# One expert's early block widened from 128 to 160 rows, and the next expert's weight loads and splits issued at other places

## The chip, the cores and the metric

The kernel runs on one core of a Trainium2 chip. The metric is device time in microseconds (us). A core has five engines with a queue each: TensorE (PE in the profile, its weight loads PEld), VectorE (DVE), ScalarE (ACT), GpSimd (POOL) and SyncE (SP), which issues most of the DMA transfers here. Times below are counted from the start of the profiled span.

## The reference

Attention with a local window and a few global keys (2 x 8 heads, 768 positions, head size 64) feeds a dense block, `g = h * tanh(softplus(h))` between a 512 x 2048 and a 2048 x 512 matrix, and that feeds a mixture of eight experts, which is the part that the change touches:

```python
logits = x @ w_gate                          # 1536 tokens, 8 experts
expert_idx = np.argmax(logits, axis=1)
for e in range(E):
    mask = expert_idx == e
    xe = x[mask]
    h = np.maximum(xe @ w1[e], 0.0)          # 512 -> 1024
    ye = h @ w2[e]                           # 1024 -> 512
    out[mask] = gate_w[mask, None] * ye
```

## The kernel before

The tokens stand in six blocks of 256. While the dense block works on its last pass, each finished block is routed: a small product with `w_gate`, a rank within the expert, and two indirect DMAs (scatters, L578) that write the block's rows into the table `xg` in DRAM, sorted by expert. Then the experts run one after another, the fullest first. Each has a fixed capacity, `CAPS = [336, 288, 256, 224, 208, 200, 184, 176]` rows.

The work on experts is a list of stages, `STG`: (expert by rank, first row, rows). The first expert has two stages, an early one of the first `EARLY = 128` rows and one of the other 208; each further expert has one. The fullest expert is fixed after the fifth block, so the early stage starts before the sixth and last block is routed: its rows of the table are there already. The second stage needs rows of the last block, so its loads (`b_xload(1)`) wait for the last scatters.

A stage has eight steps m. `b_L1(g, m)` multiplies the rows by a 128-wide slice of the expert's first matrix and takes the relu; `b_L2(g, m - 2)` multiplies the result by the slice of the second matrix, two steps later (`LAG = 2`). `b_xload` loads the stage's rows (tile `xr`), and `b_xprep` transposes them on TensorE (`btp`) and copies them to `xc`. Stage 0 multiplies in plain float32 with unsplit weights (tile `w0f`), and its relu result is `hf`. All later stages use weights and rows split into a high and a low part: a load (`b_raw`, tile `bst`, eight chunks of 512 KB for an expert), then `b_conv`, which for each of a chunk's two halves casts the high part on ScalarE (L154) and subtracts on VectorE (L155). In a stage of fewer than 256 rows a product is a pair of matmuls: the high weights times high and low rows side by side (L710, 2 x rows columns), and the low weights times the high rows (L711). Then the relu piece takes four instructions: ScalarE copy `t`, VectorE add `t`, ScalarE relu `hc`, VectorE subtract `hc`. `b_yevac` and `b_yout` take the sums out of PSUM, transpose them back (`ytp`) and scatter them to `out`.

A scheduler turns this program order into one queue per engine: an instruction that is ready sooner by its estimate may be put ahead of an earlier one. `tc.issue_after(ins)` puts what its block contains behind `ins`; it acts on the instructions of the engine that `ins` is on, and on no other. Tiles called `xr`, `x` (the routed rows of a block) and `z` share three buffers.

Of the kernel before, what the change touches and what calls it, by code (L numbers as in the profile page):

```python
# [1 line left out]

# [6 lines left out]
F32 = mybir.dt.float32  # L9
# [22 lines left out]
CAPS = [336, 288, 256, 224, 208, 200, 184, 176]  # L32
CAPMAX = max(CAPS)
NWARM = 12
EARLY = 128
ROW = DM + 2
NOID = 65536.0
ERS = NT + 128
# [3 lines left out]
def moe_kernel(ctx, tc, q, k, v, n_global, n_local, w_in, w_out, w_gate, w1, w2, out, dbg=None):  # L42
# [544 lines left out]
    def route_step(blk):  # L587
        if blk not in rsteps:
            rsteps[blk] = route_steps([xes.pop(2 * blk), xes.pop(2 * blk + 1)], ps,
                                      [wk.tile([128, 4, 128], F32, tag="cv", name="xt") for _ in range(2)])  # L590
        sc = next(rsteps[blk], None)
        if sc and blk >= NBLK - 2:
            tc.declare_no_dep(sc[1].ins, sc[0].ins, reason="disjoint rows")
            xdep[:] = [x.ins for x in sc]
# [47 lines left out]
    def b_reg(r):  # L642
        src = permt[0][0:1, r:r + 1] if r else perm0
        ereg[r] = nc.sync.value_load(src, min_val=0, max_val=NE - 1)
# [16 lines left out]
    def b_conv(r, i):  # L661
        which, f, kk = CH[i]
        if kk == 0:
            pool, tag = (wp, "w") if nsw[0] % 6 != 3 else (wlate[0], "w2")
            nsw[0] += 1
            sw[r, which, f] = [pool.tile([128, 4, 512], F32R, tag=tag, name="bw") for _ in range(2)]
        hi, lo = sw[r, which, f]
        st = braw.pop((r, i))
        for k2 in range(2):
            kx = 2 * kk + k2  # L670
            split(st[:, k2, :], hi[:, kx, :], lo[:, kx, :])

    def b_xload(g):
        r, o, cap = STG[g]
        nt = (cap + 127) // 128
        rows = []
        for i in range(nt):
            n = min(128, cap - i * 128)
            xr = xe.tile([128, ROW], F32, tag="x2", name="xr")
            ld = nc.sync.dma_start(xr[0:n], xg[bass.ds(ereg[r] * ERS + o + i * 128, n), :])  # L680
            if g < 2:
                for d in xdep:
                    tc.add_manual_dep(ld.ins, d.name, mybir.DependencyInfo(
                        mybir.DependencyClass.Sync, mybir.DependencyReason.DATA), reason="rows of the scatter")
            rows.append((xr, n))
        bx[g] = rows
# [28 lines left out]
            nc.tensor.matmul(o[:, 0:cap], lhsT=wl, rhs=xh, start=False, stop=last)  # L715

    hcs = {}
    bacc = {}

    def b_L1(g, m):  # L720
        r, _, cap = STG[g]
        cat = cap < 256
        xc = bx[g][2]
        hp = ps.tile([128, 512], F32, tag="b", name="bhp")
        if g == 0:
            hf = wk.tile([128, cap], F32, tag="gh", name="hf", bufs=3)
            for kk in range(4):
                nc.tensor.matmul(hp[:, 0:cap], lhsT=w0f[1, m // 4][:, kk, (m % 4) * 128:(m % 4) * 128 + 128],
                                 rhs=xc[:, kk, :], start=(kk == 0), stop=(kk == 3))
            nc.scalar.activation(out=hf, in_=hp[:, 0:cap], func=AF.Relu)  # L730
            hcs[g, m] = hf
            return
        wh, wl = sw[r, 1, m // 4]
        cs = slice((m % 4) * 128, (m % 4) * 128 + 128)
        for kk in range(4):
            mm3(hp, cap, cat, wh[:, kk, cs], wl[:, kk, cs], xc[:, kk, 0, :], xc[:, kk, 1, :],
                xc[:, kk].rearrange("p a c -> p (a c)"), kk == 0, kk == 3)
        if cat:
            hc = wk.tile([128, 2, cap], F32R, tag="gh", name="hc", bufs=3)
            hh, hl = hc[:, 0], hc[:, 1]  # L740
            hc = hc.rearrange("p a c -> p (a c)")
            t1 = wk.tile([128, cap], F32, tag="e", name="t1")
            nc.scalar.copy(t1, hp[:, cap:2 * cap])
            nc.vector.tensor_add(t1, t1, hp[:, 0:cap])
            src = t1
        else:
            hc = None
            hh = wk.tile([128, cap], F32R, tag="gh", name="hh", bufs=3)
            hl = wk.tile([128, cap], F32R, tag="gl", name="hl", bufs=3)
            src = hp[:, 0:cap]  # L750
        nc.scalar.activation(out=hh, in_=src, func=AF.Relu)
        nc.vector.scalar_tensor_tensor(out=hl, in0=src, scalar=0.0, in1=hh.bitcast(F32),  # L752
                                       op0=ALU.max, op1=ALU.subtract)
        hcs[g, m] = (hh, hl, hc)

    def b_L2(g, m):
        r, _, cap = STG[g]
        cat = cap < 256
        if m == 0:
            bacc[g] = [ps.tile([128, 512], F32, tag="b", name="bacc") for _ in range(4)]  # L760
        if g == 0:
            hf = hcs.pop((g, m))
            for d in range(4):
                nc.tensor.matmul(bacc[g][d][:, 0:cap], lhsT=w0f[2, m // 4][:, m % 4, d * 128:(d + 1) * 128],
                                 rhs=hf, start=(m == 0), stop=(m == 7))
            return
        hh, hl, hc = hcs.pop((g, m))
        wh, wl = sw[r, 2, m // 4]
        for d in range(4):
            mm3(bacc[g][d], cap, cat, wh[:, m % 4, d * 128:(d + 1) * 128],  # L770
                wl[:, m % 4, d * 128:(d + 1) * 128], hh, hl, hc, m == 0, m == 7)
# [347 lines left out]
    NM = 8 * len(STG)  # L1119
    LAG = 2  # L1120
    YLAG = LAG + 1
    for i in range(NM + YLAG + 1):
        g, m = divmod(i, 8)
        if i < NM:
            r = STG[g][0]
            b_L1(g, m)
            if m == 0 and g + 1 < len(STG) and STG[g + 1][0] != r:
                b_reg(r + 1)
            if m == (0 if g else 3) and g + 1 < len(STG):
                b_xload(g + 1)  # L1130
            if m == 5 and g + 1 < len(STG):
                b_xprep(g + 1)
            if g > 0 and r + 1 < NE:
                if m == 1:
                    b_raw(r + 1, 0)
                    b_raw(r + 1, 1)
                    b_raw(r + 1, 2)
                if m >= 2 and m + 1 < 8:
                    b_raw(r + 1, m + 1)
        if i >= LAG and i - LAG < NM:  # L1140
            g2, m2 = divmod(i - LAG, 8)
            b_L2(g2, m2)
            if m2 == 7:
                b_yevac(g2)
        if i == 0:
            with tc.high_priority():
                route_step(LAST)
                route_step(LAST)
                final_rank()
            routed = dsi_ins[0].ins  # L1150
        if i < 8:
            with tc.issue_after(routed):
                b_conv(0, i)
        if i < NM and g > 0 and r + 1 < NE and m >= 2:
            b_conv(r + 1, m - 2)
        if i < NM and g > 1 and m in (0, 1):
            b_conv(r, m + 6)
        if i >= YLAG and (i - YLAG) % 8 == 7:
            b_yout((i - YLAG) // 8)
# [217 lines left out]
```

## Time and profile before

| | us |
|---|---|
| median of 3 runs (lowest, highest) | 628.48 (628.40, 630.04) |
| the profiled execution, its own time | 628.33 |
| its span | 626.5 |
| TensorE busy in the span | 590.0 (94%) |
| VectorE, ScalarE, GpSimd busy | 485.2, 394.6, 90.1 |

The busy shares are means over stages with different limits. The stage to look at here lies between 400 and 455 us, where the last block is routed and the first expert's two stages run; after it TensorE is busy without a break to the last expert. The granted clock is given as a share of TensorE's full speed: 1.00 is 2.4 GHz, 0.50 is 1.2 GHz.

### The profile page before, as it was taken

What the parts mean: (1) busy time and instruction counts of PE and PEld (TensorE: products, weight loads), DVE (VectorE), ACT (ScalarE), POOL (GpSimd) and SP (SyncE); (2) the same over time, 40 slices, a digit from 0 to 9 for tenths busy, and PEclk for the clock granted to TensorE, in tenths of its full rate; (3) what the DMA queues carried; (4) which work ended last, traced back from release to release, by engine and by line L of the source; (5) the groups of instructions that cost most, each with busy time, mean ns of one, the idle gap of its engine ahead of it and who ended that gap; (6) DMA issues with size and microseconds to landing.
All of it is one profiled execution on the core that took longest, in us unless ns stands there. A gap on an engine that the chain in (4) does not pass through costs nothing.

```text
span 626.5 us, 11976 instructions
## 1 busy us (share of the span) xinstructions
PE 590.0 (94%) x4214; PEld 511.3 (82%) x4214; DVE 485.2 (77%) x1250; ACT 394.6 (63%) x965; POOL 90.1 (14%) x152
## 2 busy tenths in 40 slices
PE   5988999999999999999999999877999999999991
PEld 4555676766799999998989898677999999998991
DVE  5798998999799999867767777565875677987741
ACT  2689998989867665555565546363754566776530
POOL 2201000100000101000211201142211122221111
PEclk7599999999999999999999999996999999999996
DMA  7686655647999764431421210546667376568000
GB/s 217 204 268 190 210 175 196 208 152 259 244 308 380 230 202 149 165 101 35 132 88 52 102 35 35 176 169 219 242 236 250 103 278 218 184 240 298 30 17 20
DMA packets 54872, 109.93 MB, mean 175 GB/s; under 512 B 5674, under 2 KB 12842, under 8 KB 54802
## 3 DMA queue, kind: packets, MB, share of 16 engines
q1 hardware_dynamic: 49122, 90.18, 44.1%
q0 software_dynamic: 5680, 18.89, 9.1%
q8 instruction: 35, 0.57, 0.4%
q14 instruction: 35, 0.29, 0.1%
HBM read 84.64 MB, written 25.10 MB: 175 GB/s over the span
## 4 chain that ended last, share of the span: by engine, by line
PE 84%; DMA 5%; DVE 3%; ACT 3%; issue 2%; POOL 1%; SPq 0%; DVEq 0%; POOLq 0%; ACTq 0%
PE hp L427 23%; PE acc L446 20%; PE bacc L710 6%; PE bhp L710 6%; PE av L379 4%; PE sp L288 4%; PE bhp L711 3%; PE bacc L711 3%; PE pt L348 2%; PE pt L350 2%; DMA xg<-x,dsi 1%; PE ytp L797 1%; DMA xr<-xg 1%; PE bacc L713 1%; PE bhp L713 1%
## 5 line engine op out<-in xcount | busy, mean ns | idle before, releaser
L427 PE MATMUL hp<-xh,wpair 128*128 128x256 f32 x768 | 154.4, 288 | 1.0 <-ACT xh L391 1.0
L427 PEld LDWEIGHTS hp<-xh,wpair 128*128 128x128 f32 x768 | 122.5, 189 | 8.4 <-issue 3.6
L446 PE MATMUL acc<-wpair,gh 128*128 128x512 f32 x384 | 124.8, 401 | 1.4 <-ACT gh L483 1.4
L427 PE MATMUL hp<-xl,wpair 128*128 128x256 f32 x384 | 110.4, 288 | 0.3 <-DVE xl L396 0.3
L155 DVE TENSOR_TENSOR bw<-bst,bw 128x512 fp32r<-128x512 f32 x112 | 73.0, 685 | 11.6 <-ACT bw L154 10.6
L446 PEld LDWEIGHTS acc<-wpair,gh 128*128 128x128 f32 x384 | 68.2, 188 | 16.3 <-issue 3.5
L446 PE MATMUL acc<-wpair,gl 128*128 128x512 f32 x192 | 77.2, 403 | 0.0
L154 ACT CAST bw<-bst 128x512 fp32r<-128x512 f32 x112 | 64.6, 620 | 19.1 <-PE bhp L714 7.9
L427 PEld LDWEIGHTS hp<-xl,wpair 128*128 128x128 f32 x384 | 72.3, 188 | 5.0 <-issue 3.2
L454 ACT ACTIVATE e<-hp 128x512 f32<-128x512 f32 x48 | 28.8, 601 | 69.6 <-PE hp L427 69.6
L710 PE MATMUL bacc<-hc,bw 128*128 128x416 f32 (+4 forms) x192 | 60.1, 366 | 0.4 <-DVE hc L752 0.4
L710 PE MATMUL bhp<-xc,bw 128*128 128x416 f32 (+4 forms) x192 | 60.4, 367 | 0.0
L320 ACT ACTIVATE P<-P,mx 128x232 f32<-128x232 f32 (+1 forms) x96 | 44.8, 470 | 11.1 <-DVE mx L302 10.9
L711 PE MATMUL bhp<-xc,bw 128*128 128x208 f32 (+4 forms) x192 | 48.9, 255 | 0.0
L711 PE MATMUL bacc<-hc,bw 128*128 128x208 f32 (+4 forms) x192 | 48.8, 254 | 0.0
L464 DVE SCALAR_TENSOR_TENSOR n<-n,r 128x512 f32<-128x512 f32 x48 | 33.0, 688 | 18.7 <-ACT r L462 18.5
L302 DVE CUSTOM_DVE_ANT_0 P<-sp,ndist 128x232 f32<-128x232 f32 (+1 forms) x96 | 35.7, 374 | 10.3 <-PE sp L288 9.4
L446 PEld LDWEIGHTS acc<-wpair,gl 128*128 128x128 f32 x192 | 36.1, 188 | 9.3 <-issue 2.7
L486 DVE SCALAR_TENSOR_TENSOR gl<-n,gh 128x512 fp32r<-128x512 f32 x48 | 33.1, 689 | 11.5 <-ACT gh L483 10.6
L288 PE MATMUL sp<-kT,qT 64*128 64x232 f32 (+1 forms) x192 | 35.6, 428 | 3.1 <-DVE qT L263 3.1
L379 PE MATMUL av<-PT,vv 128*64 128x128 f32 (+2 forms) x384 | 36.0, 303 | 2.0 <-ACT PT L357 2.0
L710 PEld LDWEIGHTS bacc<-hc,bw 128*128 128x128 f32 x192 | 36.1, 188 | 1.3 <-DVE hc L752 0.6
(188 smaller groups left out, 1294.6 us busy)
## 6 DMA issues: line engine op xcount, KB each, us to landing
bst<-in_moe_w_dram SPq DMA_DIRECT2D x56, 512.0 KB
wst<-in_moe_w_in_dram SPq DMA_DIRECT2D x16, 512.0 KB
wst<-in_moe_w_out_dram SPq DMA_DIRECT2D x16, 512.0 KB
xl<-xs POOLq DMA_DIRECT2D x12, 512.0 KB, 4.1
xh<-xs POOLq DMA_DIRECT2D x12, 512.0 KB, 4.8
xpl<-xps SPq DMA_DIRECT2D x24, 256.0 KB
xg<-z SPq DMA_DIRECT2D x24, 224.9 KB
w0f<-in_moe_w_dram SPq DMA_DIRECT2D x8, 512.0 KB
```

The lines of the kernel that those rows point to most:

```text
L154: nc.scalar.copy(hi, src)
L155: nc.vector.tensor_sub(lo, src, hi.bitcast(F32))
L288: nc.tensor.matmul(sp[:, 0:w], lhsT=qT[r, p_, :], rhs=kT[r, p_, k0:k0 + w], start=True, stop=True)
L302: nc.vector.tensor_tensor_reduce(out=P[:, j, 0:w], in0=sp[j][:, 0:w], in1=ndist[:, d0:d0 + w], scale=-(2.0 ** -(h + 1)), scalar=3.0e38, op ...
L320: nc.scalar.activation(out=P[:, j, 0:w], in_=P[:, j, 0:w], func=AF.Exp, bias=mx[:, j:j + 1], scale=-1.0, accum_out=su[:, j:j + 1])
L379: nc.tensor.matmul(av[64 * j:64 * j + 64, p_, :], lhsT=lh, rhs=rh, start=(c == 0), stop=(c == 1))
L427: yield lambda f=f, kk=kk, wi=wi, xx=xx, cs=cs: nc.tensor.matmul(hp[:, f, :], lhsT=w[:, wi, kk, cs], rhs=xx[:, kk, :], start=(kk == 0 and ...
L446: yield lambda f=f, o=o, cs=cs, gi=gi, wi=wi, first=first, last=last: nc.tensor.matmul(accs[b][o], lhsT=gi[:, cs], rhs=w[:, wi, f, :], sta ...
L464: nc.vector.scalar_tensor_tensor(out=n, in0=n, scalar=0.25, in1=r, op0=ALU.add, op1=ALU.mult)
L486: nc.vector.scalar_tensor_tensor(out=gl, in0=n, scalar=-(2.0 ** -80), in1=gh.bitcast(F32), op0=ALU.mult, op1=ALU.subtract)
L710: nc.tensor.matmul(o[:, 0:2 * cap], lhsT=wh, rhs=xc, start=first, stop=False)
L711: nc.tensor.matmul(o[:, 0:cap], lhsT=wl, rhs=xh, start=False, stop=last)
```

## The change

`EARLY` is 160, so that the stages of the first expert have 160 and 176 rows in place of 128 and 208. Stage 0 is written out as a block of its own. In it the second stage's transposes (`b_xprep(1)`) stand behind all eight `b_L1` and six `b_L2`, and six of the second expert's eight weight loads are issued there; before they stood in stage 1. The splits of the second expert's weights stand in stage 1 as before, now each within `issue_after(hlast[m - 2])`, where `hlast[m]` is the VectorE instruction that ends stage 1's relu piece m.

```diff
-EARLY = 128
+EARLY = 160
...
-        nc.vector.scalar_tensor_tensor(out=hl, in0=src, scalar=0.0, in1=hh.bitcast(F32),
-                                       op0=ALU.max, op1=ALU.subtract)
+        ins = nc.vector.scalar_tensor_tensor(out=hl, in0=src, scalar=0.0, in1=hh.bitcast(F32),
+                                             op0=ALU.max, op1=ALU.subtract)
+        if g == 1:
+            hlast[m] = ins.ins
...
-    for i in range(NM + YLAG + 1):
+    def early_block():
+        for m in range(8):
+            b_L1(0, m)
+            if m == 3:
+                b_xload(1)
+            if m >= LAG:
+                b_L2(0, m - LAG)
+            if m == 0:
+                with tc.high_priority():
+                    route_step(LAST)
+                    route_step(LAST)
+                    final_rank()
+            with tc.issue_after(dsi_ins[0].ins):
+                b_conv(0, m)
+        b_xprep(1)
+        b_reg(1)
+        for i in range(6):
+            b_raw(1, i)
+        for m in range(8 - LAG, 8):
+            b_L2(0, m)
+        b_yevac(0)
+
+    early_block()
+    for i in range(8, NM + YLAG + 1):
...
-            if m == (0 if g else 3) and g + 1 < len(STG):
+            if m == 0 and g + 1 < len(STG):
                 b_xload(g + 1)
...
+                if m in (3, 4) and g == 1:
+                    b_raw(r + 1, m + 3)
...
-        if i < NM and g > 0 and r + 1 < NE and m >= 2:
-            b_conv(r + 1, m - 2)
+        if i < NM and r + 1 < NE and m >= 2:
+            with tc.issue_after(hlast[m - 2]) if g == 1 else nullcontext():
+                b_conv(r + 1, m - 2)
```

TensorE's queue at the second stage's transposes, before. `L728` is a product of stage 0's first matrix, `L764` of its second, `L697` a transpose of the second stage's rows, `L710` and `L711` that stage's first pair.

```order
L764 MATMUL bacc<-hf,w0f 128x128 x4
L697 MATMUL btp<-ident,xr 128x128 x4
L764 MATMUL bacc<-hf,w0f 128x128 x2
L697 MATMUL btp<-ident,xr 128x80 x4
L728 MATMUL bhp<-xc,w0f 128x128 x4
L764 MATMUL bacc<-hf,w0f 128x128 x2
L728 MATMUL bhp<-xc,w0f 128x128 x4
L764 MATMUL bacc<-hf,w0f 128x128 x4
L710 MATMUL bhp<-xc,bw 128x416
```

The same place in TensorE's queue now; the two kinds of product of stage 0 are `L729` and `L767` here.

```order
L729 MATMUL bhp<-xc,w0f 128x160 x4
L767 MATMUL bacc<-hf,w0f 128x160 x4
L697 MATMUL btp<-ident,xr 128x128 x4
L697 MATMUL btp<-ident,xr 128x48 x4
L767 MATMUL bacc<-hf,w0f 128x160 x8
L710 MATMUL bhp<-xc,bw 128x352
```

Of stage 0's 64 products 40 stood ahead of the transposes and 56 do now; 8 are left behind them, the last two steps of the second matrix.

ScalarE's queue at the end of stage 0, before. `L730` is the relu of stage 0, `L702` the copy of the second stage's transposed rows, `L154` a cast, of the first expert's weights where it reads `w0f` and of the second expert's where it reads `bst`.

```order
L154 CAST bw<-w0f 128x512 x2
L702 CAST xc<-btp 128x4x128
L154 CAST bw<-w0f 128x512
L702 CAST xc<-btp 128x4x80
L154 CAST bw<-w0f 128x512
L730 ACTIVATE hf<-bhp 128x128 x2
L154 CAST bw<-bst 128x512 x2
L743 COPY t_5385<-bhp 128x208
```

The same place in ScalarE's queue now (`L731` is the relu of stage 0, `L788` the copy of its sums, `L744` the first copy of stage 1's relu piece).

```order
L731 ACTIVATE hf<-bhp 128x160
L154 CAST bw<-w0f 128x512
L154 CAST bw<-bst 128x512 x2
L731 ACTIVATE hf<-bhp 128x160
L154 CAST bw<-bst 128x512 x2
L731 ACTIVATE hf<-bhp 128x160
L702 CAST xc<-btp 128x4x128
L702 CAST xc<-btp 128x4x48
L788 COPY ys<-bacc 128x160 x2
L744 COPY t_5432<-bhp 128x176
```

Four casts of the second expert's weights moved from behind the last two relus of stage 0 and the copies to `xc` to ahead of them.

SyncE's queue from the second stage's row loads, now; the second expert's loads stood behind three more `xr` loads before.

```order
L680 DMA xr<-xg 48x514
L644 TENSOR_LOAD perm
L644 ISA x2
L656 ISA
L656 DMA bst<-in_moe_w_dram 128x2x512
L656 ISA
L656 DMA bst<-in_moe_w_dram 128x2x512
L658 ISA
L658 DMA bst<-in_moe_w_dram 128x2x512
```

The weight loads now follow the second stage's own rows, and the three row loads of the second expert follow the weights.

## Rows read from the trace of the kernel before

**Rows 1.** Chain that ended last, routing of the last block (start us, us, what)

```profile
418.19 5.97 DMA xg<-x,dsi
...
424.42 2.88 DMA xr<-xg
```

**Rows 2.** TensorE's timeline (start us, us, engine, line, op, tiles, count, [idle before, releaser])

```profile
406.02 0.63 PE L697 MATMUL btp<-ident,xr 128*128 128x128 f32 x4 [1.02 <-DMA xr<-xg]
...
408.91 0.39 PE L728 MATMUL bhp<-xc,w0f 128*128 128x128 f32 x2
...
416.90 1.06 PE L764 MATMUL bacc<-hf,w0f 128*128 128x128 f32 x8
...
418.69 1.06 PE L764 MATMUL bacc<-hf,w0f 128*128 128x128 f32 x8
427.34 1.11 PE L697 MATMUL btp<-ident,xr 128*128 128x128 f32 x4 [7.60 <-DMA xr<-xg]
...
434.04 0.44 PE L710 MATMUL bhp<-xc,bw 128*128 128x416 f32 x1
...
454.64 0.31 PE L713 MATMUL bhp<-xc,bw 128*128 128x288 f32 x1
```

**Rows 3.** Stretches (us, busy of each engine, granted clock, DMA share, GB/s)

```profile
422.00:422.50 0.50, 0.00 (x0) 0.00 (x0) 0.00 (x0) 0.00 (x0) 0.05 (x1) 0.65 0.00 0
...
427.34:432.30 4.96, 4.96 (x25) 4.96 (x26) 3.19 (x6) 2.32 (x5) 1.91 (x8) 0.50 0.55 147
...
434.04:454.64 20.60, 20.60 (x147) 20.28 (x146) 16.74 (x37) 14.92 (x37) 3.63 (x5) 1.00 0.76 267
```

**Rows 4.** TensorE's waits from 434 to 615 us (us in total, times, longest)

```profile
PE bacc L710 <- DVE hc L752: 0.4, 1, 0.4
```

**Rows 5.** TensorE's timeline, pairs at 208 and 176 rows, and transposes

```profile
437.32 0.26 PE L711 MATMUL bhp<-xc,bw 128*128 128x208 f32 x1
...
441.35 0.26 PE L711 MATMUL bhp<-xc,bw 128*128 128x208 f32 x1
...
443.16 0.26 PE L711 MATMUL bacc<-hc,bw 128*128 128x208 f32 x1
...
447.18 1.40 PE L697 MATMUL btp<-ident,xr 128*128 128x128 f32 x12
...
600.08 0.24 PE L711 MATMUL bacc<-hc,bw 128*128 128x176 f32 x1
...
601.17 0.24 PE L711 MATMUL bhp<-xc,bw 128*128 128x176 f32 x1
```

**Rows 6.** SyncE's timeline, issues of row and weight loads

```profile
425.03 0.34 SPq L680 DMA_DIRECT2D xr<-xg  x1
...
430.51 0.38 SPq L656 DMA_DIRECT2D bst<-in_moe_w_dram  x1
...
431.10 0.38 SPq L656 DMA_DIRECT2D bst<-in_moe_w_dram  x1
...
431.68 0.99 SPq L658 DMA_DIRECT2D bst<-in_moe_w_dram  x2
```

**Rows 7.** SyncE's register load by its line (ns min/median/max, first to last start)

```profile
L644 SPq TENSOR_LOAD <-perm x1: 273/273/273, 425.4 to 425.4; - x1
```

**Rows 8.** ScalarE's timeline, casts of the second expert's weights

```profile
434.33 1.14 ACT L154 CAST bw<-bst 128x512 fp32r<-128x512 f32 x2 [0.57 <-DMA bst<-in_moe_w_dram]
...
435.74 0.62 ACT L154 CAST bw<-bst 128x512 fp32r<-128x512 f32 x1
...
438.05 1.14 ACT L154 CAST bw<-bst 128x512 fp32r<-128x512 f32 x2 [0.88 <-DMA bst<-in_moe_w_dram]
439.10 0.33 ACT L743 COPY t<-bhp 128x208 f32<-128x208 f32 x1
```

**Rows 9.** ScalarE's and VectorE's timelines, rows of stage 1

```profile
428.50 0.58 ACT L702 CAST xc<-btp 128x512 fp32r<-128x512 f32 x1 [8.23 <-PE btp L697]
...
429.11 0.69 DVE L703 TENSOR_TENSOR xc<-btp,xc 128x512 fp32r<-128x512 f32 x1 [7.93 <-ACT xc L702]
```

More of the change, by code (lines that the diff above doesn't have):

```diff
@@ L1 @@
-from contextlib import ExitStack
+from contextlib import ExitStack, nullcontext
 import concourse.bass as bass
@@ L717, in moe_kernel @@
     hcs = {}
+    hlast = {}
     bacc = {}
@@ L1126, in moe_kernel @@
             b_L1(g, m)
-            if m == 0 and g + 1 < len(STG) and STG[g + 1][0] != r:
+            if m == 0 and g > 1 and g + 1 < len(STG):
                 b_reg(r + 1)
-            if m == (0 if g else 3) and g + 1 < len(STG):
+            if m == 0 and g + 1 < len(STG):
                 b_xload(g + 1)
@@ L1132, in moe_kernel @@
                 b_xprep(g + 1)
-            if g > 0 and r + 1 < NE:
-                if m == 1:
+            if r + 1 < NE:
+                if m == 1 and g > 1:
                     b_raw(r + 1, 0)
@@ L1137, in moe_kernel @@
                     b_raw(r + 1, 2)
-                if m >= 2 and m + 1 < 8:
+                if m >= 2 and m + 1 < 8 and g > 1:
                     b_raw(r + 1, m + 1)
-        if i >= LAG and i - LAG < NM:
+                if m in (3, 4) and g == 1:
+                    b_raw(r + 1, m + 3)
+        if i - LAG >= 8 and i - LAG < NM:
             g2, m2 = divmod(i - LAG, 8)
@@ L1144, in moe_kernel @@
                 b_yevac(g2)
[L1145 to L1153, printed above, removed]
-        if i < NM and g > 0 and r + 1 < NE and m >= 2:
-            b_conv(r + 1, m - 2)
+        if i < NM and r + 1 < NE and m >= 2:
+            with tc.issue_after(hlast[m - 2]) if g == 1 else nullcontext():
+                b_conv(r + 1, m - 2)
         if i < NM and g > 1 and m in (0, 1):
```

## The prediction

> **What bounds the kernel now.** I read the page's busy shares first, then TensorE's timeline around the first expert, the chain of waits there, and the stretches with the granted clock. TensorE works nearly all the time, so what counts is where it waits. The largest wait behind the attention is one place: its timeline stops when the product that starts at 418.69 is through, at about 419.6, and goes on at 427.34, after 7.60 us idle, with the transposes of stage 1's rows [rows 2]. The chain says what it waits for: the second scatter of the last block (418.19, 5.97 us) and then the load of the rows that it wrote (424.42, 2.88 us) [rows 1]. The stretches show a second price: the granted clock falls in the half microsecond from 422.0, and all work from 427.34 to 432.30, 5.0 us of it, runs at 0.50, which is 1.2 GHz; from 434.04 it is 1.00 again [rows 3]. From there to the end TensorE has no break to speak of: in stage 1 it is busy for all of the 20.60 us from 434.04 to 454.64, and one wait of 0.4 us for a relu piece stands later [rows 3, 4]. Hence what is gained or lost up to stage 2's first matmul, at 454.64 before, should reach the end nearly whole.
>
> **Wider early block.** The starts at 416.90 and 418.69 lie 16 records of stage 0's products apart: 0.112 us a record, two records a product, 0.224 us for 128 columns [rows 2]. No row shows 160 columns of this kind. Bounds: nothing more, if the pace is set by something that each record costs whatever its width (transposes of 128 and 32 rows come at 1.40 / 12 = 0.117 us each alike [rows 5]), or in proportion, 0.280 us. I take the proportion, because the pairs of the later stages get shorter with fewer columns. The Trainium skill (FP8 and Floating Point Precision, TensorE Precision Notes) says that true float32 takes four passes through the array; by it 32 more columns would add an estimated 0.053 us a product, close to the upper bound; no run here shows the width yet.
>
> TensorE now runs 56 products ahead of the transposes in place of 40. Before, 40 products (8.96 us) and the router's small products filled 408.91 to 419.6, so the router's share is 1.7 us. Now: 56 x 0.280 = 15.7, plus 1.7, from about 409.3: done at 426.7 (423.5 by the lower bound). That is before the rows can be there, so the width costs nothing on the path: the wait for the rows hides it, and only the last 8 products (2.2 us) are left behind it.
>
> **The early rows come in two tiles.** Four more transposes (0.12 us each [rows 5]) stand before the dense block's last matmuls, and with these the last block's routing, its scatters and the rows of stage 1 move by the same 0.4 us. The second tile's load may cost up to 0.6 more, the spacing of two such issues (424.42 to 425.03 [rows 1, 6]); its 32 rows follow 128 that TensorE already waited 1.02 us for [rows 2]. I take 0.4: rows there at 427.7, transposes of 128 and 48 rows (8 x 0.117) done at 428.7. The wait ahead of them is 1.0 us, in place of 7.6.
>
> **What is late next.** The second expert's first loads leave SyncE behind the second row load. That was issued at 425.03 and a register load followed at 425.4, 0.27 us long [rows 6, 7]; with the 0.4 of above it ends at 426.1, and an issue takes another 0.4 (0.38 [rows 6]): first chunk issued at about 426.5, the second 0.6 later (430.51 to 431.10). Before, the first took from 430.51 to the cast at 434.33, 3.8 us, and the second at most 4.6 us (431.10 to 435.74) [rows 6, 8]. So they land at about 430.3 and by 431.7.
>
> These landings did not matter before. Now ScalarE's queue has their four casts ahead of the last two relus of stage 0 and of the copies to `xc`; the hold acts on VectorE's half of the split alone. That ScalarE does not look past a waiting cast is seen before: the casts at 438.05 waited 0.88 us for their chunk, and the copy behind them started at 439.10, as the casts ended, though the matmuls that it copies were through at 437.6 [rows 5, 8]. The Trainium skill (TensorE: Matmul & The Clock Gate, Architectural detail) calls the queues of ScalarE and VectorE strict FIFO, which speaks against this change; by a queue that is not, the time would be that of the third rival below, and the trace agrees with the page.
>
> Step by step, a pair of casts being 1.14 us, a relu some 0.2 (a copy of more columns 0.33 [rows 8]), and the copy and subtraction of the rows 0.6 and 0.7 [rows 9]: casts of the first chunk 430.3 to 431.4, relu 6 at 431.6; casts of the second 431.7 to 432.8, relu 7 at 433.0; copies to `xc` until 433.8 and VectorE behind them: stage 1 can start at 434.4. TensorE idles from 428.7 to 431.6, then has two times 1.1 us of stage 0 to do.
>
> **Shorter stage 1.** Pairs start 1.81 / 6 = 0.302 us apart at 208 rows and 1.09 / 4 = 0.273 at 176 [rows 5]. Of 64 pairs 56 lie ahead of stage 2's first matmul: 15.3 us, with 12 transposes of the next rows (1.4) and eight of the way back (0.6): 17.3 us from stage 1's start. Before, the 20.60 us held these and the last 8 products of stage 0. The last 8 pairs save 0.2 more. VectorE was busy 16.74 of the 20.60 us [rows 3], gets 0.7 us of extra output scaling and loses about 0.6 in narrower pieces, so it has 16.8 to do in 17.3 us and what it may finish later; I cost it at nothing, and up to 1 us if that cover is too thin.
>
> **Sum at full clock.** Stage 2 starts at 434.4 + 17.3 = 451.7, against 454.64: 2.9, and 0.2: 3.1 us less, 625.2 us from the profiled execution's 628.33.
>
> **The clock.** Before, it fell some 2.5 us into the idle time and came back 5.0 us after work resumed [rows 2, 3]. Now two idle times of 1.0 and 2.9 us have 1.0 us of transposes between them. If it falls in the second, TensorE does the two steps at half speed, 431.6 to 436.0, and has full speed from 436.6: as if stage 1 had started at 436.3. That leaves 1.2 us of gain: 627.1. If it does not fall, 625.2 stands. The idle time is about as long as the one that was enough before, so I take the middle, 626.1; by the median, 0.15 above the profiled execution, 626.2.
>
> **Rivals.**
> - Weights land sooner. The row load, of half the bytes, took 2.88 us [rows 1]. If the chunks do too, relu 6 comes at 430.7, the idle time is 2.1 us, shorter than the time after which the clock fell, and stage 1 starts at 433.3: 4.2 us less, 624.1. For it speaks that fewer row loads run beside them, against it that a chunk has twice the bytes of the row tile.
> - Weights land late: slower than before. With six chunks in the air the third one took 6.4 us before (431.68 to 438.05 [rows 6, 8]). If the first now takes that, it lands at 432.9, relu 6 comes at 434.2 and, at half clock, stage 1 starts as if at 438.9: stage 2 at 456.2, less 0.2, is 1.4 us later, 629.7. It decides from a first landing some 5.0 us after issue. Against it: the first chunk has no other chunk ahead of it.
> - The hold keeps the casts back on ScalarE as well, or it looks past them. Then relus 6 and 7 are done early, TensorE goes on from the transposes at 428.7 to the last 8 products and starts stage 1 at 430.9 at full clock: stage 2 at 448.2, 6.6 us less, 621.7. The queue's order speaks against it.
>
> **How the numbers follow.** The held casts, 625.2 to 627.1, have 0.62, early weights 0.18, late weights 0.16, casts out of the way 0.04. A change of 0.3%, 1.9 us, is about what a measurement of this kernel can tell from none. Faster by more: 0.58 of the first case, all of the second and fourth: 0.58. Slower by more needs over 630.4, beyond the third case's 629.7: 0.05. Within: 0.37. The range leaves out the fourth case, a little of the second and most of the third: 623.4 to 628.8. The likeliest case's own range is 625.0 to 627.3.
>
> **What would show it.** In the changed profile the 7.60 us wait for `xr` should be about 1 us, with 56 products ahead of it, at 0.28 us each. A new wait of about 3 us should stand between the transposes and the next product, released by the relu `hf`, and ScalarE should show a wait for `bst` with the relu and the copies right behind the casts. Stage 1's first pair should start between 434 and 436.5, its pairs 0.27 us apart, and stage 2 between 451.5 and 453.6. The clock should be 0.50 for less time than the 10 us of before. It is wrong if TensorE goes on from the transposes without a wait for `hf`, if stage 1 loses time to VectorE, or if the rows of the last block come over 1 us later.

## The result, and the profile after

The changed kernel takes 623.47 us (median of 20 runs; 628.36 before, of 20). The ratio of the two is 0.9912, with a 95% interval of 0.9884 to 0.9939: by the ratio 5.5 us less, between 3.8 and 7.3. The forecast was 626.2, 2.2 us less. Medians here are of all runs; the ratios leave the slow ones out.

Executions of both kernels spread over several microseconds: their profiles have spells of different length in which the granted clock stands at 1.2 GHz, in the first 80 us, in attention work that the change doesn't touch. The profiled execution of the changed kernel, 627.95 us long, has one from 36.5 to 49 us that the profile of before lacks. So this document compares one stretch that lies behind these spells: from the last block's first transposes (`tp`, L533) to stage 2's first matmul. TensorE's timeline of the kernel before, and then of the changed one, has it so:

```profile
407.72 1.35 PE L533 MATMUL tp<-ident,x 128*128 128x128 f32 x8
```

```profile
413.56 0.60 PE L533 MATMUL tp<-ident,x 128*128 128x128 f32 x4
...
429.84 1.25 PE L729 MATMUL bhp<-xc,w0f 128*128 128x160 f32 x8
430.93 1.25 PE L767 MATMUL bacc<-hf,w0f 128*128 128x160 f32 x8
432.02 0.97 PE L697 MATMUL btp<-ident,xr 128*128 128x128 f32 x8
433.59 2.64 PE L767 MATMUL bacc<-hf,w0f 128*128 128x160 f32 x16 [0.60 <-ACT hf L731]
436.35 0.43 PE L710 MATMUL bhp<-xc,bw 128*128 128x352 f32 x1
...
450.30 0.43 PE L710 MATMUL bhp<-xc,bw 128*128 128x352 f32 x1 [0.53 <-DVE bw L155]
```

Stage 2 starts at 454.64 before [rows 2] and at 454.72 now, so the stretch is 46.92 us before and 41.16 now: 5.76 less, as much as the runs measured. The wait of 7.60 us for `xr` [rows 2] is gone altogether: the transposes follow the products without a gap. A wait of 0.60 us for `hf` is new, and one of 0.53 in stage 1 for VectorE's subtraction of weights.

The clock does not fall. The stretches of the changed kernel (TensorE, its weight loads, VectorE, ScalarE, GpSimd busy; granted clock; DMA) show 1.00 where it was 0.50 for five microseconds before [rows 3], and 0.50 only in the spell near the start:

```profile
36.50:49.00 12.50, 12.35 (x52) 8.78 (x51) 8.33 (x36) 5.38 (x18) 1.23 (x2) 0.50 0.56 182
...
426.00:433.59 7.59, 6.99 (x54) 6.70 (x52) 4.89 (x10) 3.23 (x9) 2.10 (x4) 1.00 0.74 228
436.35:454.72 18.37, 17.84 (x132) 17.34 (x133) 15.37 (x35) 11.30 (x30) 4.18 (x12) 1.00 0.72 236
```

The chain that ended last answers to [rows 1]: the second scatter's piece is 4.70 us long in place of 5.97, and behind it stands the weight load for `bst` in place of the rows' load. The rows' load now ends while TensorE still has products:

```profile
419.98 1.18 POOL xg L578
421.16 0.30 issue
421.46 4.70 DMA xg<-x,dsi
...
428.22 3.90 DMA bst<-in_moe_w_dram
```

Why the rows are sooner stands in GpSimd's timeline, which the prediction did not read. Before, the two scatter instructions of the last block are these:

```profile
414.32 3.56 POOL L578 DMA_INDIRECT xg<-x,dsi  x1 [7.95 <-issue]
418.19 3.86 POOL L578 DMA_INDIRECT xg<-x,dsi  x1 [0.30 <-issue]
```

In the changed kernel:

```profile
419.98 1.18 POOL L578 DMA_INDIRECT xg<-x,dsi  x1 [7.41 <-DVE dsi L577]
421.46 2.52 POOL L578 DMA_INDIRECT xg<-x,dsi  x1 [0.30 <-issue]
```

7.42 us have become 3.70, and the edit does not name these instructions. The experiments ask why.

ScalarE's queue behaves as forecast: the casts wait for their chunk, and relu and copies stand behind them.

```profile
432.20 1.14 ACT L154 CAST bw<-bst 128x512 fp32r<-128x512 f32 x2 [4.36 <-DMA bst<-in_moe_w_dram]
433.25 0.29 ACT L731 ACTIVATE hf<-bhp 128x160 f32<-128x160 f32 x1
433.49 1.14 ACT L154 CAST bw<-bst 128x512 fp32r<-128x512 f32 x2
434.53 0.30 ACT L731 ACTIVATE hf<-bhp 128x160 f32<-128x160 f32 x1
434.73 0.80 ACT L702 CAST xc<-btp 128x512 fp32r<-128x512 f32 x2
```

### The profile page after: what moved, and what is told of

Same layout as the page of the kernel before. It is cut to its first block, busy times and chain, and to the rows that moved or that the text cites. A ratio compares the mean times of both kernels' runs of the same rounds, so it can differ in the third digit from the quotient of the medians.

```text
span 625.7 us, 12000 instructions
## 1 busy us (share of the span) xinstructions
PE 596.0 (95%) x4222; PEld 514.8 (82%) x4222; DVE 484.8 (77%) x1251; ACT 394.9 (63%) x966; POOL 82.7 (13%) x155
## 4 chain that ended last, share of the span: by engine, by line
PE 78%; DVE 7%; DMA 6%; ACT 4%; issue 3%; POOL 1%; SPq 0%; DVEq 0%; POOLq 0%; ACTq 0%
PE hp L427 23%; PE acc L446 20%; PE av L379 4%; PE sp L288 4%; PE bhp L710 4%; PE bacc L710 4%; DMA bst<-in_moe_w_dram 3%; DVE bw L155 2%; PE pt L348 2%; PE bhp L711 2%; PE pt L350 2%; PE bacc L711 2%; PE bhp L713 1%; PE bacc L713 1%; PE bacc L715 1%
## 5 line engine op out<-in xcount | busy, mean ns | idle before, releaser
L427 PE MATMUL hp<-xh,wpair 128*128 128x256 f32 x768 | 156.3, 291 | 0.4 <-ACT xh L391 0.3
L427 PEld LDWEIGHTS hp<-xh,wpair 128*128 128x128 f32 x768 | 124.2, 191 | 8.5 <-issue 3.8
L155 DVE TENSOR_TENSOR bw<-bst,bw 128x512 fp32r<-128x512 f32 x112 | 73.1, 686 | 11.4 <-ACT bw L154 10.7
L154 ACT CAST bw<-bst 128x512 fp32r<-128x512 f32 x112 | 64.5, 620 | 21.1 <-PE bhp L714 9.6
L710 PE MATMUL bhp<-xc,bw 128*128 128x352 f32 (+4 forms) x192 | 59.4, 364 | 0.6 <-DVE bw L155 0.5
L710 PE MATMUL bacc<-hc,bw 128*128 128x352 f32 (+4 forms) x192 | 59.3, 364 | 0.2 <-DVE hc L753 0.2
L711 PE MATMUL bhp<-xc,bw 128*128 128x176 f32 (+4 forms) x192 | 48.4, 252 | 0.0
L711 PE MATMUL bacc<-hc,bw 128*128 128x176 f32 (+4 forms) x192 | 48.3, 252 | 0.0
L288 PE MATMUL sp<-kT,qT 64*128 64x232 f32 (+1 forms) x192 | 37.1, 439 | 2.9 <-DVE qT L263 2.9
L710 PEld LDWEIGHTS bhp<-xc,bw 128*128 128x128 f32 x192 | 36.1, 188 | 1.7 <-DVE bw L155 0.7
```

The costliest lines, as they stand in the source:

```text
L154: nc.scalar.copy(hi, src)
L155: nc.vector.tensor_sub(lo, src, hi.bitcast(F32))
L288: nc.tensor.matmul(sp[:, 0:w], lhsT=qT[r, p_, :], rhs=kT[r, p_, k0:k0 + w], start=True, stop=True)
L427: yield lambda f=f, kk=kk, wi=wi, xx=xx, cs=cs: nc.tensor.matmul(hp[:, f, :], lhsT=w[:, wi, kk, cs], rhs=xx[:, kk, :], start=(kk == 0 and ...
L710: nc.tensor.matmul(o[:, 0:2 * cap], lhsT=wh, rhs=xc, start=first, stop=False)
```

## The experiments

In all of them "the stretch" is the one above, and "scatters" are the GpSimd durations of the last block's two L578.

| kernel | scatters, us | wait for `xr`, us | stretch, us | median, ratio to before (95%) |
|---|---|---|---|---|
| before, again | 3.56, 3.86 | 7.8 | 46.85 | 628.42, 0.996 (0.992 to 1.000) |
| changed, again | 1.17, 2.51 | 0 | 41.31 | 625.96, 0.992 (0.988 to 0.997) |
| changed, EARLY 128 | 3.55, 7.47 | 7.3 | 47.92 | 629.57, 1.000 (0.997 to 1.004) |
| before, EARLY 160 | 1.18, 2.52 | 2.2 | 43.16 | 626.54, 0.995 (0.991 to 1.000) |
| before, `cnt` ahead of `dsi` | 3.50, 3.85 | 7.1 | 47.07 | 628.95, 1.002 (0.998 to 1.005) |
| changed, `dsi` ahead of `cnt` | 4.06, 7.47 | 4.7 | 50.25 | 631.96, 1.004 (1.001 to 1.007) |
| before, L155 held for the scatters | 0.97, 0.98 | 1.7 + 0.2 | 41.02 | 623.80, 0.993 (0.990 to 0.997) |
| changed, L155 held for the scatters | 0.98, 0.98 | 0 | 39.94 | 621.61, 0.989 (0.986 to 0.992) |
| the last one, EARLY 128 | 0.97, 0.98 | 0 | 41.89 | 623.45, 0.990 (0.986 to 0.995) |
| changed, casts held on ScalarE | 1.17, 2.52 | 0 | 41.11 | 624.52, 0.990 (0.985 to 0.995) |
| changed, no hold | 1.17, 2.52 | 0 | 42.92 | 630.44, 0.997 (0.991 to 1.004) |
| changed, late weight loads | 1.17, 2.52 | 0 | 42.25 | 625.93, 0.995 (0.990 to 1.000) |
| changed, L155 held behind `flag` | 0.97, 0.98 | 0 | 40.33 | 622.83, 0.991 (0.988 to 0.994) |
| changed, third time | 1.17, 2.52 | 0 | 41.51 | 620.78, 0.988 (0.985 to 0.991) |
| changed, L155 held behind `rank` | 0.97, 0.98 | 0 | 39.97 | 622.18, 0.989 (0.984 to 0.994) |

The stretch repeats within 0.35 us for one kernel (46.92 and 46.85; 41.16, 41.31 and 41.51), where medians of the same kernel move by five (620.78 to 625.96); so the stretch decides.

**Both kernels again.** No edit.

> The kernel before again, for a second profile. Theory A (the two last scatters are long because VectorE's subtractions of weights, L155, run beside their descriptor work on GpSimd): the subtractions run there again, so the two L578 instructions take 3 to 4 us each again, and TensorE waits 7 to 8 us for the rows of stage 1. Rival C (their length is chance of an execution): one or both come out near 1.0 to 1.5 us, and the wait is 3 to 6 us. Time 628.4 by both, within 2.

> The changed kernel again, for a second profile. Theory B (the change itself makes the scatters short, by what VectorE does beside them): 1.2 and 2.5 us again, rows of stage 1 there 2.8 us before TensorE is through with the early block, no wait for them. Rival C (chance): 3 to 4 us each in this profile, then the rows come 2 to 3 us later relative to the products, and TensorE waits 0 to 1 us for them. Time 623.5, within 2.

Each kernel has its own lengths of the scatters, the same to 0.01 us in every profile; chance is out. What VectorE does beside them is the thing to look at. In the kernel before, profiled again, these are the subtractions L155 and the small instructions of the ranking around the scatters (start, duration):

```profile
415.71 0.67 DVE L155 TENSOR_TENSOR bw<-w0f,bw 128x512 fp32r<-128x512 f32 x1
416.31 0.20 DVE L1089 TENSOR_TENSOR cmp<-rank,io 1x64 f32<-1x64 f32 x1
...
417.10 0.15 DVE L1097 CAST perm<-permf 1x8 int32<-1x8 f32 x1
417.17 0.67 DVE L155 TENSOR_TENSOR bw<-w0f,bw 128x512 fp32r<-128x512 f32 x1
...
419.87 0.67 DVE L155 TENSOR_TENSOR bw<-w0f,bw 128x512 fp32r<-128x512 f32 x1
```

GpSimd's timeline of the same execution:

```profile
413.68 3.56 POOL L578 DMA_INDIRECT xg<-x,dsi  x1 [7.96 <-issue]
417.54 3.86 POOL L578 DMA_INDIRECT xg<-x,dsi  x1 [0.31 <-issue]
```

The first scatter ends at 417.24, 0.86 us after the subtraction that ends at 416.38 and leaves VectorE to small instructions for 0.8 us. The second ends at 421.40, 0.86 after the end (420.54) of the last subtraction in the row. So a scatter seems to stand still while subtractions follow each other, and to need 0.86 us from the first pause.

**Width and order apart.** `EARLY = 128` in the changed kernel, and 160 in the kernel before.

```diff
-EARLY = 160
+EARLY = 128
```

> The changed kernel with EARLY = 128: the order of the block, the early weight loads and the hold stay, stages of 128 and 208 rows. The early block is then 56 products of 0.224 us, 2.7 us less than at 160, and stage 1's 56 pairs ahead of stage 2 take 1.6 us more, its transposes and copies 0.4 more. Theory A+ (the gain comes from more products ahead of the transposes, whatever their width): the wait for rows is 2 to 4 us in place of 0, stage 2 starts 1.5 to 3 us later than in the changed kernel, 625 to 626.5. Rival (width carries the gain): 627.5 to 628.5, as before.

```diff
-EARLY = 128
+EARLY = 160
```

> The kernel before with EARLY = 160 alone: transposes of stage 1's rows, weight loads and splits stand where they stood. 40 products of 0.272 us are ahead of the transposes, 1.9 us more than at 128; stage 1 has narrower pairs, 1.6 us less. Theory A+ (places in the order carry the gain): the wait falls from 7.6 to 5 or 6 us, and with stage 1 shorter by 1.6 to 2 us but the early block's last 16 products longer by 0.8 at half clock, 625.5 to 627. Rival (width carries the gain): 623 to 624.5.

Both kernels at 128 have long scatters, both at 160 the short ones; the new order alone is 1.0 us worse than before, and the width alone brings 3.7 us. My first theory, that places in the order carry the gain, is false as it was put. In the changed kernel at 128 the second scatter takes 7.47 us:

```profile
414.13 3.55 POOL L578 DMA_INDIRECT xg<-x,dsi  x1 [7.96 <-issue]
417.99 7.47 POOL L578 DMA_INDIRECT xg<-x,dsi  x1 [0.30 <-issue]
```

VectorE ends its subtractions there with seven in a row:

```profile
420.32 4.28 DVE L155 TENSOR_TENSOR bw<-w0f,bw 128x512 fp32r<-128x512 f32 x7
```

They end at 424.60, and the scatter at 425.46: 0.86 us again.

**Two small instructions exchanged.** At 160 `cnt` stands ahead of `dsi` in VectorE's queue, at 128 behind it. The exchange in the kernel before (core of the edit), and its reverse in the changed one:

```diff
-        dsi_ins[0] = nc.vector.tensor_copy(dsi, dst)
+        if n_done[0] == NBLK - 1:
+            kins = expert_key()
+        else:
+            kins = None
+        n_done[0] += 1
+        with tc.issue_after(kins) if kins is not None else nullcontext():
+            dsi_ins[0] = nc.vector.tensor_copy(dsi, dst)
```

> The kernel before with two small VectorE instructions exchanged: cnt (L614) stands ahead of the cast dsi, as it does in the changed kernel, and the subtraction of weights L155 comes right behind dsi. Nothing else moves. Theory A (the length of the last scatters hangs on how their GpSimd instructions fall between VectorE's subtractions): the two take 1.2 and 2.5 us in place of 3.6 and 3.9, rows come 3 to 4 us sooner, the wait of 7.6 falls to 3.5 to 4.5, stage 2 starts 3 us sooner or more: 624 to 625.5. Rival (the exchange is of no account, the width of the early block matters otherwise): 3.6 and 3.9 us, 628.4.

```diff
     def final_rank():
-        expert_key()
+        with tc.issue_after(dsi_ins[0].ins):
+            expert_key()
```

> The changed kernel with the same two exchanged the other way: dsi, then cnt, then L155, as in the kernel before. Theory A: the scatters take 3.6 and 3.9 us, or more; rows of stage 1 come 3.5 to 4.5 us later than in the changed kernel, TensorE waits 0.5 to 1.5 us for them, the second expert's weights follow as much later and with them the relu hf: TensorE waits 2 to 4 us there, stage 2 starts 2.5 to 5 us later, 626 to 628. Rival: 1.2 and 2.5 us, 624 to 626 as the changed kernel.

In the kernel before it does nothing: there my expectation is false. In the changed kernel one place of an instruction of 0.15 us makes the stretch 9 us longer, far more than the 2.5 to 5 us expected. GpSimd:

```profile
420.16 4.06 POOL L578 DMA_INDIRECT xg<-x,dsi  x1 [7.42 <-DVE cnt L614]
424.53 7.47 POOL L578 DMA_INDIRECT xg<-x,dsi  x1 [0.30 <-issue]
```

VectorE beside it, the subtraction ahead of its small instructions and the last seven:

```profile
422.69 0.67 DVE L155 TENSOR_TENSOR bw<-w0f,bw 128x512 fp32r<-128x512 f32 x1
...
426.85 4.28 DVE L155 TENSOR_TENSOR bw<-w0f,bw 128x512 fp32r<-128x512 f32 x7
```

They end at 423.36 and 431.13, the scatters at 424.22 and 432.00: 0.86 and 0.87 us later. TensorE's waits then are these (us in total, times, longest):

```profile
PE btp L697 <- DMA xr<-xg: 4.7, 1, 4.7
PE bacc L767 <- ACT hf L731: 2.5, 1, 2.5
```

The second is the wait that the prediction forecast for the change, casts held by their chunks in front of `hf`, with 2.5 us for the 2.9 that it gave. The clock falls too, but in the wait for the rows: the transposes behind it take 1.71 us, 0.97 in the changed kernel.

```profile
437.04 1.71 PE L697 MATMUL btp<-ident,xr 128*128 128x128 f32 x8 [4.68 <-DMA xr<-xg]
```

From these transposes to stage 1 it is 8.44 us at a granted clock of 0.50, where the changed kernel needs 4.33. So the 9 us are 4.8 us to the transposes, 4.1 to stage 1 and 0.1 in it.

**No subtraction beside the scatters.** A small memset on GpSimd behind both scatters, a copy of it on VectorE, and stage 0's splits behind that copy; in both kernels.

```diff
-            routed = dsi_ins[0].ins
+                pz = const.tile([1, 1], F32, name="pz")
+                pq = const.tile([1, 1], F32, name="pq")
+                with tc.issue_after(xdep[0]), tc.issue_after(xdep[1]):
+                    nc.gpsimd.memset(pz, 0.0)
+                quiet = nc.vector.tensor_copy(pq, pz)
+            routed = quiet.ins
```

> The kernel before with VectorE's subtractions of the first expert's weights held until GpSimd is through with both last scatters (a small memset on GpSimd behind them and a copy of it on VectorE). Only the small instructions of the final ranking run beside the scatters. Theory A: the two take 1.0 to 1.3 us each, rows come 5 us sooner, the wait falls from 7.6 to 2 to 3 us; the subtractions end 3 us later, which stage 1 may feel. 623 to 625.5. Rival (the length has nothing to do with the subtractions): 3.6 and 3.9, and 628 to 630.

> The changed kernel with the same hold of the subtractions. Theory A: scatters of 1.0 to 1.3 us, the second one 1.3 us shorter than in the changed kernel, rows and weights 1.2 us sooner; the wait for hf (0.6 to 0.8 us) goes, and stage 2 starts up to 0.8 us sooner, unless the subtractions, 2.7 us later, are late for stage 1 (then up to 1 us later). Within 1 us of the changed kernel. Rival: scatters unchanged at 1.2 and 2.5 us, time up to 1 us more.

The scatters take 0.97 to 0.98 us. GpSimd's timeline, and the wait for the rows, in the kernel before with the hold:

```profile
417.60 0.97 POOL L578 DMA_INDIRECT xg<-x,dsi  x1 [7.94 <-issue]
418.88 0.98 POOL L578 DMA_INDIRECT xg<-x,dsi  x1 [0.30 <-issue]
```

```profile
424.97 0.66 PE L697 MATMUL btp<-ident,xr 128*128 128x128 f32 x4 [1.72 <-DMA xr<-xg]
```

With this hold alone the kernel before gains 5.83 us of the stretch, about as much as the whole change brought: 5.91 up to the transposes and 1.88 from there to stage 1, where the clock now stays at 1.00, less 1.96 that stage 1 is longer. On top of that, the change's own wide block, early loads and hold bring 1.08. Theory A holds; the changed kernel gains more by it (1.2 to 1.6 us of the stretch) than the 0.8 expected.

**The same with 128 rows.** The last kernel with `EARLY = 128`.

> The changed kernel with EARLY = 128 and with the first expert's subtractions held until GpSimd is through with the last scatters. Theory A (what sets the gain is the scatters' length; the width matters only through the time that its products cover): scatters of 0.98 us each, 56 products of 0.224 us end 3 us before those of 160 columns, a wait of 0 to 1.5 us for the rows, stage 1 with pairs of 0.302 us; stage 2 starts 45 to 46.5 us after the dense block's last group, against 44.8 with 160. 622.5 to 624.5. Rival (the width itself is what counts): 626 and more.

With equal scatters the stretch is 1.95 us longer at 128. TensorE is through with the narrower products sooner, and then waits for `hf` and `xc`:

```profile
PE bacc L767 <- ACT hf L731: 1.7, 1, 1.7
PE bhp L710 <- DVE xc L703: 1.5, 1, 1.5
```

Up to stage 1 the two kernels take the same (21.55 and 21.53 us); the difference lies in stage 1, and most of it is the clock. After these two waits it is 0.50 from 429.0 to 432.2, and pairs start 0.56 us apart where they start 0.30 apart before and after:

```profile
429.37 0.59 PE L710 MATMUL bhp<-xc,bw 128*128 128x416 f32 x1
...
429.93 0.59 PE L710 MATMUL bhp<-xc,bw 128*128 128x416 f32 x1
```

At half the pace an estimated 1.6 of these 3.2 us are lost; by this estimate the width would be worth some 0.4 us without the fall.

**The parts of the rest.** The casts of the second expert held on ScalarE too:

```diff
-        nc.scalar.activation(out=hh, in_=src, func=AF.Relu)
+        act = nc.scalar.activation(out=hh, in_=src, func=AF.Relu)
+        if g == 1:
+            hact[m] = act.ins
...
-                b_conv(r + 1, m - 2)
+                with tc.issue_after(hact[m - 2]) if g == 1 else nullcontext():
+                    b_conv(r + 1, m - 2)
```

> The changed kernel with the second expert's casts held on ScalarE too, each behind the relu hc of stage 1's piece m - 2, so that no cast that waits for a weight chunk stands ahead of the last two relus of stage 0 and the copies to xc. Theory A (after the short scatters the queue on ScalarE costs only the 0.6 to 0.8 us that TensorE waited for hf): this wait goes, stage 2 starts 0.6 to 1.2 us sooner, 622.5 to 623.5. Rival (the casts come late for the second expert and VectorE's splits follow): stage 2 starts later or waits stand in it, 624 to 626.

No hold on the splits:

```diff
-            with tc.issue_after(hlast[m - 2]) if g == 1 else nullcontext():
+            with nullcontext():
```

> The changed kernel without the hold of the second expert's subtractions behind stage 1's relu pieces; the early loads, the block and EARLY = 160 stay. Four subtractions of 0.67 us stand ahead of VectorE's part of xc then, and wait for the same chunks as ScalarE's casts. Theory A (VectorE's part of xc is late): stage 1 starts 1 to 3 us later and part of it is given back in stage 1, where the subtractions are done already; 624 to 626. Rival (the hold is worth nothing): within 0.7 us of the changed kernel in the stretch from the dense block's end to stage 2. Scatters of 1.2 and 2.5 us by both.

The weight loads of the second expert where they were before:

```diff
-        b_reg(1)
-        for i in range(6):
-            b_raw(1, i)
...
-                if m == 1 and g > 1:
+                if m == 1:
```

> The changed kernel with the second expert's weight loads issued in stage 1, where the kernel before had them. Theory A (the early loads only bring the wait for hf, and stage 1's own length is set by TensorE's pairs and VectorE): no wait for hf, stage 1 starts 0.8 to 1.5 us sooner, and stage 2 0 to 1.5 us sooner or up to 1 us later if the last chunks are late: 622.5 to 624.5. Rival (the early loads carry a part of the gain): waits for bw in stage 1 or at stage 2's start of 2 us and more, 625.5 to 627.

The first removes the wait for `hf` and gains nothing (41.11): TensorE then waits in stage 1 for VectorE, 1.7 us for `t`, and 1.3 us for `hc` behind the stretch, between 500 and 560 us. The second costs 1.6 us, by a wait of the size expected:

```profile
431.94 0.43 PE L710 MATMUL bhp<-xc,bw 128*128 128x352 f32 x1 [2.38 <-DVE xc L703]
```

The third costs 0.9 us: no wait for `hf`, but 1.8 us for `hc` and 0.8 for `t` in stage 1. So the hold earns 1.6 us of the stretch and the early loads 0.9, and TensorE waits for VectorE in stage 1 when weights come later.

**Who is held.** Stage 0's splits behind `flag`, and behind `rank`:

```diff
-            with tc.issue_after(dsi_ins[0].ins):
+            with tc.issue_after(flagins[0]):
                 b_conv(0, m)
```

> The changed kernel with the first expert's subtractions L155 held behind the cast flag, the last small instruction of the final ranking, in place of behind dsi: no instruction is added, the 15 small ones run alone on VectorE for about 3 us. Theory A (a scatter's GpSimd instruction advances only while no L155 runs): two scatters of 0.98 us, the first 0.28 us after dsi, both through before the first L155; from the last block's first transposes to stage 2 39.9 to 40.2 us, against 41.2 in the changed kernel and 46.9 before; 622 to 622.7, below the changed kernel by 1.0 to 1.5. Rival (the fence with GpSimd's memset, not the absence of L155, made the scatters short): 2.5 us or more for one, 41 us and more.

> The changed kernel once more, to be compared with the one above on the same chip: scatters of 1.17 and 2.51 us, 41.2 us from the last block's first transposes to stage 2, 0.88% below the kernel before.

> The changed kernel with the subtractions held behind rank (L1091), so that the first L155 starts about 0.5 us after the first scatter's GpSimd instruction has begun, and in the middle of it; eight small instructions follow, then L155 without a break. It asks who is held when the scatter came first. Theory A (GpSimd is held whenever an L155 runs, whoever came first): the first scatter takes 0.95 plus the 0.67 of that L155, 1.6 us, the second falls into the small instructions and then into L155 for a part of its time, 1.0 to 8 us. Rival (whoever came first keeps going): the first scatter takes 0.98 us, and the L155 is longer than 0.67 by what it had to wait.

Without an added instruction the scatters are as short as with the fence. The hold behind `rank` says more: a subtraction stands in the middle of the first scatter, and neither is longer for it.

```profile
416.22 0.67 DVE L155 TENSOR_TENSOR bw<-w0f,bw 128x512 fp32r<-128x512 f32 x1
```

```profile
415.80 0.97 POOL L578 DMA_INDIRECT xg<-x,dsi  x1 [7.42 <-DVE key L1088]
417.08 0.98 POOL L578 DMA_INDIRECT xg<-x,dsi  x1 [0.31 <-issue]
```

Both expectations for it are wrong in part: the scatter that came first keeps going, and the subtraction isn't held either. So what is held off seems to be a scatter's beginning; this one place is all that shows it. The two kernels are 1.2 and 1.5 us shorter in the stretch than the changed kernel beside them, but their medians (622.83 and 622.18, against 620.78) don't show it: their profiles reach the stretch later, at 410.12 and 409.38 us in place of 406.36. No version here is measurably faster than the changed kernel.

## Why the prediction was wrong in size

The direction held, and the median lies 0.07 us inside the range, below the likeliest case's own 625.0 to 627.3; the gain was forecast 3.3 us too small. On the three cuts of the stretch:

- **To the transposes of stage 1's rows.** 19.62 us before, 18.46 now. The step that failed is this one: "with these the last block's routing, its scatters and the rows of stage 1 move by the same 0.4 us", and so "rows there at 427.7". The scatters did not move as they were, they became 3.72 us shorter, and the rows were there some 3 us before TensorE was through with its 56 products. The wait was 0, not 1.0.
- **From there to stage 1.** 6.70 us before, 4.33 now; the prediction had 6.7 at full clock and the worth of 8.6 with the clock's fall. ScalarE's queue, the loads' 3.8 us (3.90 measured) and the casts ahead of `hf` were right, but all of it started with the rows' loads, and so came with them: the wait for `hf` is 0.60 in place of 2.9, and the clock stays at 1.00. With scatters of 4.06 and 7.47 us, the same queue gave 2.5, and 8.44 us for this cut.
- **Stage 1.** 20.60 before, 18.37 now, 17.3 forecast. Pairs of 0.272 us were right; VectorE, costed at nothing and "up to 1 us if that cover is too thin", took a 0.53 us wait; the rest of the 1.1 is TensorE's own, which is busy for 17.84 of the 18.37 us.

The first two gave 3.5 us that the prediction at full clock did not have (and 1.9 more where it let the clock fall), the third took 1.1 back. Products of 160 columns were right: groups of eight records, four products, start 1.087 us apart, 0.272 a product, between the 0.224 and 0.280 of the bounds and near the proportion. The first rival's time, 624.1, is the nearest to the measured one, and as it says the clock does not fall; but its reason, loads that land sooner after their issue, did not hold (3.90 us). The third rival's 621.7 rests on casts out of the way, and the queue on ScalarE was in order, as forecast.

How much of the gain is luck can be estimated from the changed kernel with `dsi` ahead of `cnt`. With scatters as long as before, 4.11 us shorter in sum than there (7.42 for 11.53), its stretch would be 46.1 us at most, against 46.92. So with the scatters that the prediction counted on, the edit would have gained some 0.8 us or more, where the likeliest case had 1.2 to 3.1; the rest of the 5.76 us came from the scatters, at which neither the edit nor the prediction aimed. That the forecast had the way right rests on the first part, and the size of the gain on the second, which is luck.

The rows of before held the clue. [Rows 1] gives the second scatter as one DMA piece of 5.97 us; GpSimd's own instruction is 3.86 of it, against 0.97 to 1.33 for the ten of the earlier blocks, of which this row is the shortest:

```profile
395.63 0.97 POOL L578 DMA_INDIRECT xg<-x,dsi  x1 [13.72 <-DVE key L616]
```

The Trainium skill (SBUF — State Buffer, SBUF: two separate sides) tells of something like it: GpSimd, which writes the descriptors of its DMAs, and VectorE share a pair of ports, and while VectorE runs an operation in a two-port mode GpSimd cannot write them, so that the DMA appears blocked. L155 has two inputs in SBUF, which the Trainium skill names only against GpSimd operations that read SBUF. The runs agree that GpSimd is kept waiting by L155; which of its accesses waits, no run here shows. The Trainium skill has a blocked DMA wait until about 115 ns behind the end of the VectorE operation. The 0.85 to 0.87 us here are counted to the scatter's end and have its own work in them, so the two figures are not of the same moment. The runs differ in that a subtraction issued in a running scatter held neither (the Trainium skill has the loser blocked for the whole instruction).

What stays open: the pauses between two subtractions are a tenth of a microsecond or less, and the long scatters went through several of them without coming to an end. The first scatter of the changed kernel did not. VectorE beside it:

```profile
419.54 0.17 DVE L577 CAST dsi<-dst 128x2 int32<-128x2 f32 x1
419.62 0.69 DVE L155 TENSOR_TENSOR bw<-w0f,bw 128x512 fp32r<-128x512 f32 x1
420.23 0.15 DVE L616 SCALAR_TENSOR_TENSOR key<-cnt,rev 1x8 f32<-1x8 f32 x1
420.30 0.67 DVE L155 TENSOR_TENSOR bw<-w0f,bw 128x512 fp32r<-128x512 f32 x1
```

It ended at 421.16, 0.85 us after the end of the first L155 at 420.31, with the next one already running. So it was let in at that pause, and that is what makes it 1.18 us where it is 4.06 with `cnt` and `dsi` exchanged, though the exchange moves the subtractions by less than 0.1 us against it. Short pauses let scatters in elsewhere too: two of the earlier blocks of the kernel before (1.20 us from 331.23 and 1.16 from 355.35) end 0.89 us after the end of another 128 x 512 VectorE instruction, with the next one 0.03 to 0.04 us behind it. Why this pause let it in, and not the others, is not settled. How the width reaches the scatters is seen in part only. At 160 columns the small instructions stand in another order, and the first scatter starts 0.27 us after the end of `dsi`. In each of the six profiles at 128 columns it is 0.77 or 0.78 us: there GpSimd's queue stands in a semaphore instruction of the scatter's line for 7.5 us (before from 406.1 to 413.6, as `dsi` ends), and the scatter starts 0.7 us after it. With `cnt` and `dsi` exchanged at 128 that is still so, and the exchange did nothing there.

## What to carry to other kernels

Before moving work, look at each instruction on the critical chain against the same instruction elsewhere in the trace: a scatter that takes 3.9 us in one place and 1.0 in another may have a neighbour that slows it, and removing the neighbour (here: holding VectorE's subtractions for 3 us, 5.8 us gained) may be worth more than covering the wait. A change whose gain hangs on such a phase can lose it by the next edit, as the exchange of two small instructions showed (9 us). A wait that hangs on a load must be costed from where the load's own chain starts, since a chain that gets shorter takes the later waits with it.

## What was not expected of the hardware

- An indirect scatter's instruction on GpSimd takes 0.97 us with no such work beside it and 1.2 to 7.5 us beside back-to-back subtractions of two 128 x 512 tiles on VectorE; it then ends 0.85 to 0.87 us after the end of one of them (in the eight cases of four kernels that were read).
- Once it has begun, a subtraction beside it costs neither anything (0.97 and 0.67 us, in the kernel with the hold behind `rank`). A small cast beside the second scatter there took 0.39 us, 0.15 elsewhere.
- A copy of two columns on GpSimd (`meta`, L704) is kept in the same way: 0.19 us alone, 1.72 us from 429.23 in the changed kernel, beside seven subtractions that end at 430.89, 0.06 us ahead of it.
